# Tanh-capped attention and a gated MLP on one core: a new hand-written order of issue

## The chip, the cores and the metric

The kernel runs on one core of a Trainium2 chip. The metric is device time in microseconds, the median of several runs: 720.66 us for the kernel before (three runs, 720.16 to 720.66). Everything is float32; the products of the MLP use float32 split into two halves.

## What is computed

Attention over 8 batches, 12 heads, 448 positions and 64 columns per head, with scores capped by a tanh, and then an MLP whose gate mixes the positions:

```python
scores = cap * np.tanh(scale * np.matmul(q, k.transpose(0, 1, 3, 2)) / cap)
attn = np.exp(scores - np.max(scores, axis=-1, keepdims=True))
attn = attn / (np.sum(attn, axis=-1, keepdims=True) + 1e-09)
x = heads side by side of np.matmul(attn, v)        # 448 x 768 per batch
h = np.maximum(x @ w_in, 0.0); u, v = h[..., :512], h[..., 512:]
v_n = (v - mean(v)) / np.sqrt(var(v) + 1e-06)
v_s = np.einsum('ts,bsd->btd', w_spatial, v_n) + b_spatial[None, :, None]
out = (u * v_s) @ w_out
```

## The kernel before

The work is cut into 24 "quads" of four heads (three per batch) and 8 MLP batches. A function builds a list of 2823 steps (`plan.tasks`), each with an engine (T is TensorE, A ScalarE, V VectorE, P GpSimd, S the load queue on SyncE), the steps it depends on and the buffers it takes. Then a tuple, `ORDER`, lists the numbers of the steps in the order in which they are issued:

```python
    order = [plan.tasks[i] for i in ORDER] if bounded else plan.order()
    with tc.manual_schedule():
        for t in order:
            for u in t.allocs:
                make(u)
            t.fn()
```

Each engine works through its own steps strictly in that order; a step that waits (for another step's result, or for a buffer that is still in use) holds everything behind it on its engine. This holds for loads too: all of them are issued from SyncE, and a load whose buffer is not free holds the loads behind it.

What a quad does, by the names in the code (function `quad_bnd`): two raw loads (q and k of two head pairs, `raw`, four buffers) and two v loads; seven score steps `sc` (T, line 737, into one of two PSUM score banks `ps_s`); a `tanh` for each (A, line 741), which frees the bank; four exponentials `exp` (A, line 748); four `pv` steps (T, line 758, into the one `ps_x` bank), freed by a copy `xev` (A, line 764). VectorE folds the exponentials to a maximum (`red1`, `red2`, line 776; transpose 784; reduce `red3`, line 786). ScalarE shifts the result between partitions (`shift`, line 792), and small steps and loads over DRAM bring the reciprocals back. For the first four quads TensorE also sums the exponentials (`ones`, line 804). VectorE scales and splits the result into `xg` tiles (lines 839 and 489).

An MLP batch has 88 TensorE steps: u (lines 895 to 897), v (917 to 922), gate (986 to 991), output (1011 to 1013), with their copies and splits on ScalarE and VectorE. The output of the chip is stored by SyncE.

Weights come as int64 words and are converted on VectorE and ScalarE (`split_f64`, lines 555 to 569 and 489, 493): six steps behind each load. Blocks of w_in use one of three `w` buffers, and the first four of the six steps hold it; blocks of w_out use an `xg` buffer; rows of w_spatial come into one of three `wy` buffers (`split_f32`, load at line 514, cast at line 520). Before the list begins, the program has issued quad 0's raw loads and the first w_in block (lines 1043 to 1050), so steps 183, 184 and 0 issue nothing.

The numbers in `ORDER` that are spoken of later:

| number | step | engine |
|---|---|---|
| 7, 14, 21, 35 | loads of w_in blocks; 8 to 13, 15 to 20, 22 to 27 and 36 to 41 are the conversions | S; V, A |
| 18 | fourth conversion step of block 14 | V |
| 162, 169, 176 | loads of w_out blocks; 163 is the first conversion step of the first | S; V |
| 84, 85 | first load of w_spatial, its cast | S, V |
| 185, 186; 244 | v loads of quad 0; first v load of quad 1 | S |
| 242, 243; 301, 302 | raw loads of quad 1; of quad 2 | S |
| 246; 205 | first score step of quad 1; last one of quad 0 | T |
| 215, 216 | reduce of quad 0's maximum, its shift | V, A |
| 261, 265 | tanh 5 and 6 of quad 1 | A |
| 476, 480 | low half of batch 0's last gated tile; the output step that uses it | V, T |

Of the kernel before, what the change touches and what calls it, by code (L numbers as in the profile page):

```python
# [215 lines left out]
def gpc(n):  # L216
# [54 lines left out]
ORDER = (183, 184, 14, 0, 185, 187, 7, 186, 189, 188, 35, 243, 1, 242, 190, 2, 3, 191, 193, 195, 4, 15, 16, 17, 18, 84, 5, 194, 6,  # L271
# [137 lines left out]
def attn_moe(ctx, tc, bounded, shared, qk, v, qk2, v2, cap, w_in, w_sp, w_out, out):  # L409
# [613 lines left out]

    order = [plan.tasks[i] for i in ORDER] if bounded else plan.order()
    with tc.manual_schedule():
# [76 lines left out]
```

## Time and profile before

| | before |
|---|---|
| median of 3 runs | 720.66 us |
| profiled execution: its time, its span | 719.57 us, 717.3 us |
| TensorE busy | 706.5 us (98%) |
| VectorE busy | 594.6 us (83%) |
| ScalarE busy | 476.6 us (66%) |
| GpSimd busy | 25.8 us (4%) |
| granted TensorE clock | 1.00 |
| moved by DMA | 66.57 MB |

The span runs from the first to the last instruction of the profiled execution; a little lies around it. A busy time counts an engine's own instructions, waits left out. Matmuls overlap, so TensorE's steps are read by when they start. Starts in the views below are in microseconds from the start of the span.

### The profile page before, as it was taken

How to read it: one execution, taken by the hardware profiler on the slowest of the kernel's cores; microseconds unless marked ns; L12 is line 12 of the kernel's file. 1: busy time of each engine (PE TensorE's matmuls, PEld its weight loads, DVE VectorE, ACT ScalarE, POOL GpSimd, SP SyncE). 2: the span in 40 equal slices, each digit the busy share in tenths (PEclk: the TensorE clock that was granted, in tenths of full speed). 3: DMA queues.
4: the chain of work that ended last, by engine and by line, in shares of the span. 5: the costliest groups of instructions: out<-in, count | busy, mean ns of one | idle time of the engine just before them, and what ended most of it. 6: DMA issues, size and time to landing. Idle time of an engine off the chain costs nothing.

```text
span 717.3 us, 12273 instructions
## 1 busy us (share of the span) xinstructions
PE 706.5 (98%) x4954; PEld 483.0 (67%) x4954; DVE 594.6 (83%) x868; ACT 476.6 (66%) x646; POOL 25.8 (4%) x45
## 2 busy tenths in 40 slices
PE   8999999999999999999999999999999999999997
PEld 2334658665765958658676956667859666689896
DVE  6999999999999788999767499999768898793430
ACT  6999956787676576884475768687375874733321
POOL 0000010000200000000100010100000000000100
PEclk9999999999999999999999999999999999999999
DMA  8745415433031303323113411414104321202002
GB/s 288 245 135 175 164 42 161 126 104 119 12 104 52 130 9 122 93 76 118 51 42 89 155 37 57 141 52 128 66 27 116 103 71 48 65 1 79 27 1 82
DMA packets 34511, 66.57 MB, mean 93 GB/s; under 512 B 5995, under 2 KB 22156, under 8 KB 34444
## 3 DMA queue, kind: packets, MB, share of 16 engines
q1 hardware_dynamic: 34444, 65.68, 28.8%
q8 instruction: 41, 0.67, 0.4%
q14 instruction: 26, 0.21, 0.1%
HBM read 54.45 MB, written 11.18 MB: 92 GB/s over the span
## 4 chain that ended last, share of the span: by engine, by line
PE 79%; DVE 12%; ACT 7%; issue 1%; DMA 1%; ACTq 0%; DVEq 0%
PE ps_x L758 13%; PE ps_s L737 13%; PE ps_acc L895 4%; PE ps_acc L897 4%; PE ps_acc L896 4%; PE ps_acc L1011 4%; DVE red L776 4%; PE ps_acc L1012 4%; PE ps_acc L1013 4%; ACT tp L741 3%; PE ps_acc L920 3%; PE ps_acc L921 3%; PE ps_acc L922 3%; PE ps_acc L989 2%; ACT tp L748 2%; PE ps_acc L991 2%
## 5 line engine op out<-in xcount | busy, mean ns | idle before, releaser
L741 ACT ACTIVATE tp<-ps_s,capt 128x896 f32<-128x896 f32 x168 | 164.8, 1007 | 40.0 <-PE ps_s L737 36.1
L748 ACT ACTIVATE tp<-tp,capt 128x1792 f32<-128x1792 f32 x96 | 153.3, 1607 | 0.8
L737 PE MATMUL ps_s<-raw 64*64 64x448 f32 x1344 | 149.0, 545 | 3.0 <-ACT tp L741 2.9
L758 PE MATMUL ps_x<-tp,v 64*64 64x448 f32 x1344 | 141.2, 537 | 0.3 <-ACT xf L764 0.3
L776 DVE TENSOR_TENSOR red<-red,tp 128x1792 f32<-128x1792 f32 x88 | 136.3, 1549 | 5.5 <-ACT tp L748 3.7
L758 PEld LDWEIGHTS ps_x<-tp,v 64*64 64x64 f32 x1344 | 50.6, 133 | 76.0 <-issue 70.7
L737 PEld LDWEIGHTS ps_s<-raw 64*64 64x64 f32 x1344 | 46.7, 133 | 78.0 <-issue 41.9
L776 DVE TENSOR_TENSOR red<-tp 128x1792 f32<-128x1792 f32 x44 | 88.7, 2016 | 7.9 <-ACT tp L748 7.3
L895 PE MATMUL ps_acc<-xg,wi_h 128*128 128x448 f32 x180 | 66.2, 368 | 0.0
L897 PE MATMUL ps_acc<-xg,wi_l 128*128 128x448 f32 x180 | 65.2, 362 | 0.0
L896 PE MATMUL ps_acc<-xg,wi_h 128*128 128x448 f32 x180 | 65.0, 361 | 0.0
L1011 PE MATMUL ps_acc<-xg,wo_h 128*128 128x448 f32 x176 | 64.7, 368 | 0.0
L1012 PE MATMUL ps_acc<-xg,wo_h 128*128 128x448 f32 x176 | 63.8, 362 | 0.0
L1013 PE MATMUL ps_acc<-xg,wo_l 128*128 128x448 f32 x176 | 63.5, 361 | 0.0
L920 PE MATMUL ps_acc<-wi_h,xg 128*128 128x512 f32 x126 | 49.8, 395 | 0.1
L784 DVE STREAM_TRANSPOSE red<-red 128x896 f32<-128x896 f32 x44 | 48.6, 1104 | 0.9
L922 PE MATMUL ps_acc<-wi_h,xg 128*128 128x512 f32 x126 | 49.1, 390 | 0.0
L921 PE MATMUL ps_acc<-wi_l,xg 128*128 128x512 f32 x126 | 49.1, 390 | 0.0
L776 DVE TENSOR_TENSOR red<-red 128x896 f32<-128x896 f32 x44 | 47.8, 1087 | 0.5
L944 POOL TENSOR_TENSOR lst<-lst,capt 128x1 f32<-128x1 f32 x32 | 24.8, 782 | 650.5 <-DVE lst L942 570.1
L786 DVE TENSOR_REDUCE st<-red 128x28 f32<-128x896 f32 x44 | 47.5, 1079 | 0.6
L493 ACT COPY o<-ps_acc 128x448 f32<-128x448 f32 x44 | 23.2, 533 | 36.6 <-PE ps_acc L1013 34.0
(150 smaller groups left out, 1060.0 us busy)
## 6 DMA issues: line engine op xcount, KB each, us to landing
raw<-in_qk SPq DMA_DIRECT2D x46, 448.0 KB
rr<-rd SPq DMA_DIRECT2D x48, 224.0 KB
out<-o SPq DMA_DIRECT2D x48, 224.0 KB
v<-in_v SPq DMA_DIRECT2D x24, 256.0 KB
w<-in_w_in SPq DMA_DIRECT2D x11, 512.0 KB
v<-in_v SPq DMA_DIRECT2D x24, 192.0 KB
xg<-in_w_out SPq DMA_DIRECT2D x12, 256.0 KB
rd<-dt SPq DMA_DIRECT2D x48, 3.5 KB
```

What stands on the lines that cost most here:

```text
L737: nc.tensor.matmul(ps.t[c * D:(c + 1) * D, e, :S], lhsT=f(raw[c].t)[r, k:k + D], rhs=f(raw[c].t)[r, :S], start=True, stop=True)
L741: th = add("A", act(PW, 1), kk("th", i), lambda ps=ps, tp=tp, o=o: nc.scalar.activation(out=tp.t[:, o:o + PW].rearrange("p (e q) -> p e q" ...
L748: ex = add("A", act_s(w, 1), kk("ex", i), lambda tp=tp, w=w: nc.scalar.activation(out=tp.t[:, :w], in_=tp.t[:, :w], func=AF.Exp, scale=ca) ...
L758: nc.tensor.matmul(x.t[e * D:(e + 1) * D, c, :S], lhsT=vts[g // 2].t[c * D:(c + 1) * D, (4 * (g % 2) + 2 * j + e) * D:(4 * (g % 2) + 2 * j ...
L776: nc.vector.tensor_tensor(o_(), i0(), i1(), op=op)
L895: nc.tensor.matmul(ps, lhsT=wi1_h[:, c, fs], rhs=x[:, XH:], start=(c == 0), stop=False)
L896: nc.tensor.matmul(ps, lhsT=wi1_h[:, c, fs], rhs=x[:, :S], start=False, stop=False)
L897: nc.tensor.matmul(ps, lhsT=wi1_l[:, c, fs], rhs=x[:, XH:], start=False, stop=(c == NP - 1))
L920: nc.tensor.matmul(ps, lhsT=x[:, XH:][:, ts], rhs=wi2_h[:, c], start=(c == 0), stop=False)
L1011: nc.tensor.matmul(ps, lhsT=wo_h[:, c, ns], rhs=g[:, XH:], start=(c == 0), stop=False)
L1012: nc.tensor.matmul(ps, lhsT=wo_h[:, c, ns], rhs=g[:, :S], start=False, stop=False)
L1013: nc.tensor.matmul(ps, lhsT=wo_l[:, c, ns], rhs=g[:, XH:], start=False, stop=(c == 3))
```

## The change

One tuple is replaced. No step is added, removed or altered, no buffer and no load; all 2823 numbers stand in the new tuple once, in another order. All five engines are affected: 850 of TensorE's 984 places hold another step, 783 of VectorE's 861, 559 of ScalarE's 644, 263 of the load queue's 302, 24 of GpSimd's 32. The head of the diff, with the steps of the table above:

```diff
-ORDER = (183, 184, 14, 0, 185, 187, 7, 186, 189, 188, 35, 243, 1, 242, 190, 2, 3, 191, 193, 195, 4, 15, 16, 17, 18, 84, 5, 194, 6,
-    8, 196, 19, 197, 220, 192, 201, 199, 9, 10, 20, 11, 200, 202, 12, 221, 246, 205, 198, 36, 210, 37, 85, 38, 13, 39, 86, 203,
-    247, 206, 40, 248, 222, 252, 207, 249, 253, 21, 90, 244, 87, 28, 204, 258, 208, 254, 211, 41, 212, 91, 22, 92, 213, 23, 214,
-    24, 29, 215, 30, 88, 25, 31, 89, 250, 259, 255, 260, 223, 264, 279, 256, 224, 261, 26, 209, 262, 265, 216, 169, 301, 302, 49,
...
+ORDER = (162, 176, 169, 163, 183, 184, 187, 189, 188, 190, 191, 195, 193, 14, 0, 1, 164, 2, 165, 177, 3, 15, 166, 16, 4, 194, 196,
+    5, 17, 170, 18, 19, 185, 201, 192, 21, 199, 220, 197, 200, 202, 7, 186, 35, 178, 8, 6, 20, 9, 36, 10, 37, 11, 179, 203, 221,
+    243, 242, 246, 247, 205, 198, 206, 12, 252, 248, 204, 222, 302, 301, 244, 84, 38, 210, 85, 211, 86, 207, 249, 253, 254, 208,
+    258, 223, 250, 255, 209, 259, 256, 251, 264, 260, 279, 257, 39, 22, 212, 23, 213, 24, 13, 214, 25, 40, 215, 216, 26, 224, 261,
+    265, 245, 97, 28, 49, 218, 42, 307, 305, 262, 306, 217, 266, 98, 269, 171, 27, 41, 280, 281, 311, 90, 225, 282, 263, 87, 226,
...
```

## Rows read from the trace of the kernel before

**Rows 1.** Busy time by stretch: each engine's us (instructions), TensorE's granted clock, DMA share, GB/s.

```profile
7.20:40.00 32.80, 28.95 (x327) 10.03 (x322) 32.47 (x51) 32.47 (x35) 0.00 (x0) 1.00 0.71 248
35.00:40.00 5.00, 3.82 (x44) 1.31 (x40) 5.00 (x10) 4.90 (x8) 0.00 (x0) 1.00 0.16 55
40.00:138.47 98.47, 98.46 (x830) 56.96 (x823) 96.23 (x188) 81.81 (x115) 2.50 (x4) 1.00 0.45 141
138.47:250.00 111.53, 111.03 (x763) 76.85 (x762) 105.79 (x130) 77.91 (x107) 4.65 (x4) 1.00 0.28 88
250.00:600.00 350.00, 349.93 (x2449) 240.21 (x2448) 297.44 (x389) 240.46 (x317) 13.03 (x16) 1.00 0.26 81
600.00:712.00 112.00, 112.00 (x583) 96.71 (x581) 61.88 (x107) 41.94 (x72) 4.59 (x8) 1.00 0.12 40
```

**Rows 2.** Timeline of TensorE: start, us, line, operation; in brackets idle time before it.

```profile
28.69 0.98 PE L737 MATMUL ps_s<-raw 64*64 64x448 f32 x8
...
37.66 0.98 PE L737 MATMUL ps_s<-raw 64*64 64x448 f32 x8 [1.18 <-ACT tp L741]
```

**Rows 3.** Timeline of the load queue on SyncE: when loads are issued.

```profile
7.43 0.80 SPq L719 DMA_DIRECT2D raw<-in_qk  x2
8.34 0.37 SPq L514 DMA_DIRECT2D wy<-in_w_sp  x1
11.83 0.33 SPq L555 DMA_DIRECT2D w<-in_w_in  x1
19.53 0.33 SPq L514 DMA_DIRECT2D wy<-in_w_sp  x1
...
29.70 0.33 SPq L719 DMA_DIRECT2D raw<-in_qk  x1
```

**Rows 4.** GB/s moved in each microsecond from 0 to 40.

```profile
GB/s 0 0 75 141 369 415 377 430 377 344 379 346 283 390 394 413 392 37 0 0 108 310 309 281 145 264 378 415 417 395 233 309 136 134 321 242 19 0 0 16
```

**Rows 5.** Timeline of VectorE in the first 30 us.

```profile
7.20 0.43 DVE L562 TENSOR_SCALAR red<-red 128x512 f32<-128x512 f32 x1 [2.85 <-DMA red<-in_w_in]
7.66 0.43 DVE L566 TENSOR_SCALAR red<-red 128x512 uint32<-128x512 uint32 x1
...
11.11 0.69 DVE L569 SCALAR_TENSOR_TENSOR wy<-w,wy 128x512 uint32<-128x512 uint32 x1
11.72 0.68 DVE L489 TENSOR_TENSOR wi_l<-red,wi_h 128x512 fp32r<-128x512 f32 x1
...
17.91 0.39 DVE L520 CAST ws_h<-wy 128x448 fp32r<-128x448 f32 x1
...
20.56 2.02 DVE L776 TENSOR_TENSOR red<-red,tp 128x1792 f32<-128x1792 f32 x1
...
24.40 0.43 DVE L562 TENSOR_SCALAR wy<-w 128x512 f32<-128x512 f32 x1
24.73 0.62 DVE L489 TENSOR_TENSOR ws_l<-wy,ws_h 128x448 fp32r<-128x448 f32 x1
...
28.54 1.08 DVE L786 TENSOR_REDUCE st<-red 128x28 f32<-128x896 f32 x1
```

**Rows 6.** Timelines of VectorE and TensorE at the end of batch 0.

```profile
137.86 0.61 DVE L489 TENSOR_TENSOR xg<-o,xg 128x448 fp32r<-128x448 f32 x1
...
139.11 0.36 PE L1011 MATMUL ps_acc<-xg,wo_h 128*128 128x448 f32 x1
139.32 0.36 PE L1012 MATMUL ps_acc<-xg,wo_h 128*128 128x448 f32 x1
```

**Rows 7.** Timeline of TensorE at two changes of kind of work.

```profile
48.02 1.68 PE L737 MATMUL ps_s<-raw 64*64 64x448 f32 x16
49.53 1.68 PE L758 MATMUL ps_x<-tp,v 64*64 64x448 f32 x16
...
58.28 1.73 PE L737 MATMUL ps_s<-raw 64*64 64x448 f32 x16
59.94 0.47 PE L895 MATMUL ps_acc<-xg,wi_h 128*128 128x448 f32 x1
```

243 rows, old and new, of the table ORDER are left out of this document.

## The prediction

> **What bounds the kernel now.** I read the busy time by stretch first [rows 1]. From 40 us to the last matmul TensorE is busy in 98.46 of 98.47, 111.03 of 111.53, 349.93 of 350.00 and 112.00 of 112.00 us, at a granted clock of 1.00 throughout. No new order can make that part shorter by more than these few tenths. The only stretch with room is the start: 28.95 of 32.80 us between 7.20 and 40, so 3.85 us in all, the longest hole being the 1.18 us ahead of 37.66, where TensorE waits for the tanh that frees a score bank [rows 2]. The same table shows who sets the pace there: ScalarE and VectorE are each busy 32.47 of 32.80 us. VectorE stays the fullest engine behind TensorE up to 138.47 (96.23 of 98.47 us) [rows 1]. So VectorE is idle for 0.33 + 2.24 = 2.57 us between 7.20 and 138.47. The reader is to see two things: hardly anything can be gained after 40 us, and a hole torn into VectorE's work before 138 us can hardly be filled again.
>
> Whether such a hole costs time depends on how late VectorE delivers. At the end of batch 0 it writes the low half of the last gated tile (step 476) from 137.86 for 0.61 us, so until 138.47. TensorE enters the step that uses it (480) at 139.11 and reads the low half with its second matmul at 139.32 [rows 6]. The slack is 0.85 us. I compared the two tables at this place: exactly the same 235 VectorE steps stand ahead of 476, and exactly the same 158 TensorE steps ahead of 480. Whatever idle time VectorE gains up to there reaches TensorE less 0.85 us, and behind it TensorE has nothing to win it back from.
>
> **The change, part by part.** *Middle and end.* The same steps in other runs. Changes of TensorE between attention and MLP go from 47 to 49, one pair more. Two score steps took 1.51 us between attention steps (48.02 to 49.53) and 1.66 us ahead of an MLP run (58.28 to 59.94) [rows 7]; the pair costs twice 0.15 at most, and I take 0.2 us. Up to 250 us VectorE has 5.74 us idle behind 138.47, and 52.56 us between 250 and 600 [rows 1], which covers what is swapped there. The last steps are again an output projection, its copy and its store. I count nothing else here; a new wait of a microsecond is possible and lies in the range.
>
> *The head of the load queue.* Two lines of the trace show how this queue acts. The fourth load of a w_in block (a transfer into `w`) was issued at 11.83, just when VectorE's fourth operation on an earlier block ended (11.11 + 0.69 = 11.80): there are three such buffers, and SyncE stands until one is free. The load of quad 3's q and k at 29.70 came just when quad 1's last scores ended (28.69 + 0.98 = 29.67): there are four raw buffers [rows 2, 3, 5]. In the table of before, quad 1's raw loads (243, 242) and the first w_spatial load (84) stand ahead of that fourth w_in load; they went out at 7.43 and 8.34 [rows 3]. In the new table three w_out blocks (162, 176, 169) come first, then w_in blocks 14, 21, 7, and the fourth w_in load (35) ahead of quad 1's raws. Quad 2's raws (302, 301) come next, and the w_spatial load 84 only behind them and quad 1's first v.
>
> *What VectorE meets.* I follow its new queue with the start-to-start times of the rows: 0.33 us for a 512-column operation between unrelated ones (24.40 to 24.73), 0.61 for the two-input one (11.11 to 11.72), for the 256-column ones somewhat over half of that (0.2 and 0.33, estimates), 2.02 for a first fold. Sizes are the code's: a w_out block 262 KB, a w_in block 524, raw 459, w_spatial 229, v 262 or 197. Bytes come from the rate row: with the queue full it sums to 1377 KB by 7 us, 1807 by 8, 2528 by 10, 2907 by 11 and 4320 by 15 us. The start loads are 1442 KB, and their first 1180 KB (reached at 6.5) let VectorE start at 7.20, 0.7 later [rows 4, 5].
> 1. VectorE's first step is now 163, on a w_out block: 1442 + 262 = 1704 KB, reached at 7.8, so a start at 8.4 instead of 7.20. Hole 1.2.
> 2. Step 15 needs block 14, now behind 786 KB of w_out: 2752 KB, 10.6 + 0.7 = 11.3; VectorE is there at 10.65. Hole 0.6.
> 3. Step 18, which frees the buffer for load 35, ends at 14.4 (11.80 before). Step 8 waits for block 7 (4062 KB, 15.0): hole 0.5. Load 35 goes out at 14.4; after an issue at 19.53 on an idle queue bytes flowed from about 20.7 [rows 3, 4], so its 524 KB flow from 15.6 to 17.0 at 380 KB/us, and step 36 starts at 17.7: hole 0.8.
> 4. Quad 1's raws (918 KB) follow until 19.4, so the first score step of quad 1 (246) starts at 20.0. Quad 0's last scores (205) stand behind it on TensorE: 20.75 to 21.75. Only then do quad 2's raws get their buffers; they go out at 21.8, flow from 23.0, and with v and load 84 (1409 KB) end at 26.7. Step 85, the cast of that w_spatial block, starts at 27.4. It stands in VectorE's queue directly behind quad 0's first fold, which ends at 22.4. Hole 5.0. In before, 85 ran at 17.91 with no wait [rows 5].
>
> The holes sum to 1.2 + 0.6 + 0.5 + 0.8 + 5.0 = 8.1 us. Against that, the new queue mixes two chains, so that a step seldom follows its own predecessor: 0.46 us start to start in a chain (7.20 to 7.66) against 0.33, and eight such neighbours before step 36 go away: 8 x 0.13 = 1.0. VectorE is later by 7.1 us.
>
> *Who waits for that.* Behind 85 stand the rest of quad 0's maximum, whose end (step 215, at 29.62 in before, 9.06 us after 20.56 [rows 5]) moves to about 37. ScalarE has the shift of that result (216) in front of quad 1's tanh 5 and 6 now, behind them before; so quad 1's last tanhs and the score bank that quad 2's first scores need come about 38 to 40 us. TensorE stands some 4 us there. That is the same delay seen from another engine, not added.
>
> The sum: 7.1 - 0.85 + 0.2 = about 6.4 us. The profiled execution took 719.57 us with a span of 717.3; it becomes 726.0 with a span of 723.7. The median of the runs shown is 1.09 us above the profiled execution, and I forecast on it: 720.66 + 6.4 = 727.0. Low end of this case: all 2.57 us of VectorE's old idle time fill up, 3.8 us, 724.5. High end: quad 2's transfers flow at the 281 KB/us of the slice at 23 us [rows 4] rather than 380, 5.0 instead of 3.7 us, 728.3.
>
> **The clock.** Before, the granted clock is 1.00 in the stretch from 35 to 40 too, where TensorE was busy 3.82 of 5.00 us [rows 1]; a hole as long as the new one stands in no row. [...]
>
> **The rivals.** *Faster.* If loads and holes were as before, the new order would lead ScalarE past one w_in cast less, and the tanhs ahead of some exponentials, before quad 2's scores: banks come free earlier, and of TensorE's 3.85 us of holes about half could go, 2 us: 718.7. It decides when step 84 lands before VectorE is at 85, that is by 22.4. Against it: two buffer waits in a row, both seen in the trace. *No change.* The same delay exists, but VectorE has made it up before 138: 720.7. It needs the hole at 85 to be under about 2 us, so a landing near 24; the rate row leaves no room for 1.4 MB between 21.8 and 24. [...]
>
> **How the numbers follow.** Forecast 0.73 (724.5 to 728.3), slower still 0.12, no change 0.08, faster 0.07. Two executions of this kernel can be told apart from about 0.2%, 1.4 us. So faster 0.07, same 0.08, slower 0.85. The range 723.0 to 731.0 takes in the forecast's bounds and the slower rival, and leaves out the other two.
>
> **What the new profile would show.** VectorE's first operation near 8.4 on `xg`; the fourth `w` load issued near 14.4; quad 2's raws near 21.8; VectorE idle some 5 us at the line of the cast of `wy` (520), ended by a DMA; ScalarE idle some 4 us at line 792, and TensorE idle as long before 40 us. From 45 us on TensorE is full again, step 476 ends near 145, and the rest is only shifted. Wrong would be: step 85 without a wait (then the queue doesn't hold loads as I read it); or that wait with the end of 476 near 139 (then VectorE had cover that I don't see); or a full start and a new hole after 140.

## The result and the profile after

The changed kernel takes 729.91 us, median of five runs (728.54 to 731.85), against 720.66 (720.16 to 720.90, five runs): a ratio of 1.0132, 95% interval 1.0118 to 1.0145. That is 9.25 us slower; the forecast was 6.4 us (727.0), with a range of 723 to 731. The forecast's own case was bounded by 724.5 and 728.3; 729.91 lies above it, in the part of the range that was drawn for the rival "slower still". The profiled execution took 731.43 us with a span of 729.5, against 719.57 and 717.3. It is the second slowest of the five, so the views below show a loss of 11.86 us where the medians differ by 9.25.

The busy time by stretch, in the columns of [rows 1]:

```profile
7.20:40.00 32.80, 24.85 (x262) 8.76 (x256) 20.18 (x37) 23.58 (x23) 0.00 (x0) 0.90 0.52 179
40.00:150.00 110.00, 105.92 (x884) 59.04 (x881) 107.33 (x200) 90.39 (x126) 2.39 (x4) 0.97 0.47 147
150.00:250.00 100.00, 99.92 (x709) 66.76 (x708) 96.00 (x122) 71.13 (x92) 3.08 (x4) 1.00 0.28 89
250.00:600.00 350.00, 349.87 (x2394) 245.60 (x2396) 298.78 (x388) 237.72 (x319) 9.44 (x16) 1.00 0.27 81
600.00:712.00 112.00, 112.00 (x637) 90.70 (x630) 74.45 (x119) 48.30 (x81) 4.40 (x8) 1.00 0.13 40
```

From 150 us on TensorE is as full as before. The first stretch has changed: VectorE worked 32.47 us in it and now 20.18, ScalarE 32.47 and now 23.58, TensorE 28.95 and now 24.85.

VectorE's own timeline shows where it stood (the number in brackets is the idle time ahead of the operation, and what ended it; most operations without a wait are left out):

```profile
8.53 0.29 DVE L562 TENSOR_SCALAR xg<-xg 128x256 f32<-128x256 f32 x1 [4.21 <-DMA xg<-in_w_out]
...
11.72 0.43 DVE L562 TENSOR_SCALAR wy<-w 128x512 f32<-128x512 f32 x1 [0.88 <-DMA w<-in_w_in]
...
16.00 0.43 DVE L562 TENSOR_SCALAR wy<-w 128x512 f32<-128x512 f32 x1 [0.97 <-DMA w<-in_w_in]
...
20.15 0.43 DVE L562 TENSOR_SCALAR wy<-w 128x512 f32<-128x512 f32 x1 [2.18 <-DMA w<-in_w_in]
...
22.96 2.02 DVE L776 TENSOR_TENSOR red<-tp 128x1792 f32<-128x1792 f32 x1
32.24 0.39 DVE L520 CAST ws_h<-wy 128x448 fp32r<-128x448 f32 x1 [7.25 <-DMA wy<-in_w_sp]
...
41.10 1.12 DVE L786 TENSOR_REDUCE st<-red 128x28 f32<-128x896 f32 x1
```

Every one of the waits shown ends with a transfer; of the operations in [rows 5] only the first, at 7.20, has a wait ahead of it, the cast of line 520 at 17.91 none. Besides the start (8.53 for 7.20) the holes are 0.88, 0.97, 2.18 and 7.25 us. The load queue, in the columns of [rows 3], and the GB/s of each microsecond from 0 to 40, as in [rows 4]:

```profile
14.85 0.33 SPq L555 DMA_DIRECT2D w<-in_w_in  x1
15.27 11.48 SPq L719 DMA_DIRECT2D raw<-in_qk  x4
27.66 0.33 SPq L726 DMA_DIRECT2D v<-in_v  x1
28.08 0.38 SPq L514 DMA_DIRECT2D wy<-in_w_sp  x1
```

```profile
GB/s 0 0 72 156 375 417 369 414 350 365 346 334 297 383 331 91 239 319 288 304 212 54 4 0 0 0 32 240 391 366 302 79 0 16 178 18 0 0 0 0
```

Load 35 goes out at 14.85, quad 1's raws right behind it, quad 2's raws not before some 26 (the group of four issues stretches from 15.27 to 26.75), and the w_spatial load 84 at 28.08. Between 22 and 26 us next to nothing is moved: the transfers are not slow there, the queue stands.

TensorE and ScalarE at the same place, and the granted clock around it:

```profile
22.67 3.27 PE L737 MATMUL ps_s<-raw 64*64 64x448 f32 x16 [4.48 <-DMA raw<-in_qk]
25.68 1.92 PE L758 MATMUL ps_x<-tp,v 64*64 64x448 f32 x16
...
44.32 3.26 PE L737 MATMUL ps_s<-raw 64*64 64x448 f32 x16 [4.01 <-ACT tp L741]
```

```profile
42.25 0.22 ACT L792 COPY sh<-st 32x32 f32<-32x32 f32 x1 [4.69 <-DVE st L786]
```

```profile
18.00:26.00 8.00, 3.52 (x24) 1.45 (x24) 4.84 (x7) 3.75 (x4) 0.00 (x0) 0.58 0.31 108
26.00:40.00 14.00, 13.91 (x160) 5.03 (x152) 7.76 (x11) 10.83 (x11) 0.00 (x0) 1.00 0.36 116
40.00:50.00 10.00, 5.99 (x48) 2.13 (x48) 9.74 (x12) 6.84 (x10) 0.00 (x0) 0.66 0.77 245
```

TensorE has two holes of over 4 us, and over the two score steps behind each the granted clock is 0.50 (from 22.67 to 25.68 and from 44.32 to 47.51; the means of 18 to 26 and of 40 to 50 us are 0.58 and 0.66): two score steps take 3.01 us from start to start (22.67 to 25.68), where two took 1.51 in [rows 7]. The end of batch 0, and TensorE's busy time on the way there:

```profile
150.04 0.64 DVE L489 TENSOR_TENSOR xg<-o,xg 128x448 fp32r<-128x448 f32 x1
```

```profile
151.00 0.36 PE L1011 MATMUL ps_acc<-xg,wo_h 128*128 128x448 f32 x1
151.20 0.36 PE L1012 MATMUL ps_acc<-xg,wo_h 128*128 128x448 f32 x1
```

```profile
72.00:150.00 78.00, 78.00 (x588) 49.39 (x585) 77.39 (x154) 62.51 (x91) 2.39 (x4) 1.00 0.44 136
```

Against [rows 6] step 476 ends 12.21 us later (150.68 for 138.47) and TensorE reads it 11.88 later (151.20 for 139.32). At the end the span is 12.2 us longer. From 72 us TensorE is busy without a hole, so it was as late at 72 us already: the whole loss is made in the head.

### The profile page after: what moved, and what is told of

It is laid out like the page before. It is cut to its first block, busy times and chain, and to the rows that moved or that the text cites. A ratio compares the mean times of both kernels' runs of the same rounds, so it can differ in the third digit from the quotient of the medians.

```text
span 729.5 us, 12311 instructions
## 1 busy us (share of the span) xinstructions
PE 710.5 (97%) x4954; PEld 484.1 (66%) x4954; DVE 597.5 (82%) x868; ACT 476.1 (65%) x646; POOL 20.3 (3%) x45
## 4 chain that ended last, share of the span: by engine, by line
PE 84%; DVE 8%; ACT 3%; DMA 2%; issue 1%; SPq 0%; ACTq 0%; DVEq 0%
PE ps_s L737 15%; PE ps_x L758 15%; PE ps_acc L895 5%; PE ps_acc L897 5%; PE ps_acc L896 5%; PE ps_acc L1011 4%; PE ps_acc L1012 4%; PE ps_acc L1013 4%; DVE red L776 4%; PE ps_acc L920 3%; PE ps_acc L921 3%; PE ps_acc L922 3%; PE ps_acc L989 3%; PE ps_acc L991 2%; PE ps_acc L990 2%; PE ps_acc L917 1%
## 5 line engine op out<-in xcount | busy, mean ns | idle before, releaser
L737 PE MATMUL ps_s<-raw 64*64 64x448 f32 x1344 | 150.0, 552 | 10.8 <-ACT tp L741 6.2
L748 ACT ACTIVATE tp<-tp,capt 128x1792 f32<-128x1792 f32 (+1 forms) x96 | 153.0, 1607 | 0.8
L493 ACT CAST xg<-xf 128x448 fp32r<-128x448 f32 (+1 forms) x96 | 35.3, 408 | 22.6 <-DVE xf L839 15.8
```

The source lines that it names most:

```text
L737: nc.tensor.matmul(ps.t[c * D:(c + 1) * D, e, :S], lhsT=f(raw[c].t)[r, k:k + D], rhs=f(raw[c].t)[r, :S], start=True, stop=True)
L748: ex = add("A", act_s(w, 1), kk("ex", i), lambda tp=tp, w=w: nc.scalar.activation(out=tp.t[:, :w], in_=tp.t[:, :w], func=AF.Exp, scale=ca) ...
```

## The experiments

The theory (A) is that of the forecast: VectorE's holes behind held loads in the head make the loss. The rivals are that the rest of the new table makes it, tried first, and that TensorE's and ScalarE's own holes and the clock make it; each text on record says which of them it calls B. All ratios are to the kernel before, run beside each kernel on the same chip; the chips differ from run to run (the kernel before took 720.66 to 721.65 us on them), so kernels are compared by their ratios. In the short diffs of loads, numbers stand in the order in which SyncE issues them.

**Which part of the table.** Up to the end of batch 0's gate both tables issue the same 638 steps (159 of TensorE, 236 of VectorE, 148 of ScalarE, 91 loads, 4 of GpSimd). So the head can be taken from one and the rest from the other.

```diff
-ORDER = (new head, new rest)
+ORDER = (these 638 in the old order, new rest)   # old_head_new_rest
+ORDER = (these 638 in the new order, old rest)   # new_head_old_rest
```

> Every engine runs the order of before up to the end of batch 0's gate (236 VectorE steps, 159 TensorE, 148 ScalarE, 91 loads) and the new order from there. Theory A (the whole loss is made in the first 55 us, by the load queue): 720.7 within 1.5 us, TensorE full from 40 us on as in before. Theory B (part of the loss comes from the new runs in the middle): above 723, with new holes of TensorE behind 140 us.

> The other half: the new order up to the end of batch 0's gate, the old order from there. Theory A: as slow as the changed kernel, 729 to 732, with the same 7 us wait of VectorE for a wy load near 25 to 32 us. Theory B: clearly under 728.

Measured: the old head with the new rest 719.73 us, 0.9976 (0.9964 to 0.9988); the new head with the old rest 730.51 us, 1.0129 (1.0092 to 1.0166). Both fall where theory A put them: the head alone makes the loss; the rest costs nothing that can be told. VectorE's busy time from 7.2 to 60 us, old head first (columns as in [rows 1]):

```profile
7.20:60.00 52.80, 48.39 (x555) 17.57 (x553) 50.83 (x81) 52.01 (x59) 0.00 (x0) 1.00 0.66 221
```

```profile
7.20:60.00 52.80, 41.88 (x426) 14.39 (x424) 39.64 (x66) 40.71 (x43) 0.00 (x0) 0.90 0.57 184
```

**One load at a time.** Both kernels are the changed one with loads moved ahead of load 35.

```diff
-35, 243, 242, 302, 301, 244, 84
+84, 35, 243, 242, 302, 301, 244   # load84_first
+243, 242, 35, 302, 301, 244, 84   # raws_first
```

> The new order with one load moved: the first w_spatial load (84) goes out ahead of the fourth w_in load (35); nothing else changes. If the wait of step 85 for that load is the main term (7.25 of about 12 us), VectorE has no wait at line 520, ScalarE's 4.7 us wait at line 792 and TensorE's 4.0 us hole near 40 us go away: about 724 to 725. If the late raw loads of quad 1 (TensorE's 4.5 us hole at 18 us) are the main term and 85 only follows them, the time stays above 727.

> The new order with quad 1's two raw loads (243, 242) moved ahead of load 35; load 84 stays behind quad 2's raws. Quad 1's first scores should start near 16.5 instead of 22.7, with no hole of 4.5 us and no half clock there; quad 2's raws go out near 18 instead of 26, so load 84 lands some 6 to 7 us earlier too and the wait at line 520 shrinks to under 1.5 us. Theory A, with the raws as the root: 721 to 723. If 85's wait for 84 is a cause of its own that stays: about 725.

Measured: 724.94 us, 1.0043 (1.0025 to 1.0060), and 725.51 us, 1.0052 (1.0035 to 1.0070). Each move takes away 60 to 70% of the loss. With 84 first the time is in the range given for it; VectorE casts 84 without a wait, ScalarE's wait at line 792 and TensorE's hole near 40 us are gone, and TensorE's hole ahead of quad 1 stays. With the raws first, that hole shrinks to 0.56 us, and waits behind 84 stay, shorter. There the 721 to 723 of theory A fell and the other case, "about 725", came: quad 1's scores started at 19.17 for the 16.5 expected, quad 2's raws went out at 20.93 for 18, and the wait at line 520 is 1.99 us for under 1.5. VectorE and TensorE with 84 first:

```profile
25.28 0.38 DVE L520 CAST ws_h<-wy 128x448 fp32r<-128x448 f32 x1
```

```profile
22.70 3.27 PE L737 MATMUL ps_s<-raw 64*64 64x448 f32 x16 [4.34 <-DMA raw<-in_qk]
```

VectorE, ScalarE and TensorE with the raws first:

```profile
27.12 0.40 DVE L520 CAST ws_h<-wy 128x448 fp32r<-128x448 f32 x1 [1.99 <-DMA wy<-in_w_sp]
```

```profile
37.09 0.22 ACT L792 COPY sh<-st 32x32 f32<-32x32 f32 x1 [4.38 <-DVE st L786]
```

```profile
19.17 1.73 PE L737 MATMUL ps_s<-raw 64*64 64x448 f32 x16 [0.56 <-DMA raw<-in_qk]
...
39.16 3.27 PE L737 MATMUL ps_s<-raw 64*64 64x448 f32 x16 [3.70 <-ACT tp L741]
```

**Both moves.**

```diff
-35, 243, 242, 302, 301, 244, 84
+243, 242, 84, 35, 302, 301, 244
```

> The new table with both moves of the two earlier runs: q1's raw loads 243 and 242 and then the w_spatial load 84 go out ahead of load 35; nothing else differs. Theory A (VectorE's holes behind held loads make the loss): the 7.25 us before the cast at L520 and the 2.2 us before load 35's cast go or shrink below 1, what stays is the 1.33 + 0.88 us behind the first w_in and w_out blocks and about 1 us: 3.2 less the slack of 0.85 over the 719.7 of the old head with the new rest, so about 722 (720.5 to 723). Theory B (TensorE's and ScalarE's own holes and the clock make it): no wait at L792, no hole at 40 us and no half clock are left, so 719.5 to 720.5. If something else in the new head costs (a third cause), it stays at 724 to 725.5, where each move alone left it.

Measured: 722.96 us, 1.0032 (1.0017 to 1.0046), just within the range of theory A (720.5 to 723) and outside that of B. This doesn't refute B, though: its range supposed that no hole is left near 40 us, and ScalarE still waits 2.55 us at line 792 and TensorE 1.86 us behind it. Another point missed: the hole at load 35 did not shrink, it is 2.61 us, behind the 1.1 MB that now stand ahead of that load. VectorE and TensorE:

```profile
20.57 0.43 DVE L562 TENSOR_SCALAR wy<-w 128x512 f32<-128x512 f32 x1 [2.61 <-DMA w<-in_w_in]
```

```profile
37.35 2.11 PE L737 MATMUL ps_s<-raw 64*64 64x448 f32 x16 [1.86 <-ACT tp L741]
```

**ScalarE's order alone.** The shift 216, which waits for VectorE, goes behind tanh 5 and 6 again, first in the changed kernel, then in the one with the raws first.

```diff
-216, 26, 224, 261, 265, 245
+26, 224, 261, 265, 216, 245
```

> The new table with one step moved: ScalarE's copy 216 (L792), which waits for VectorE's step 215, goes behind the tanh steps 261 and 265 again; all loads stay as the change has them. Under both theories ScalarE's 4.7 us wait ahead of tanh 5, TensorE's 4.0 us hole at 40 us and the half clock behind it go. Theory A: VectorE's holes (1.33, 0.88, 0.97, 2.18, 7.25) stay, its step ahead of the gate ends as late as before, and the time stays at 728 to 730.5. Theory B: 4.0 us of hole and 1.6 us of scores at half clock come off, 723.5 to 725.

> The run with q1's raws first (725.5), and copy 216 behind the tanh steps 261 and 265 as well. There VectorE's wait at L520 had shrunk to 1.99 us, but ScalarE still waited 4.38 us at L792 and TensorE 3.70 us behind it, at half clock for 3.41 us after. Theory A: VectorE's waits (1.3, 0.9, 1.9, 2.0, together 6.1 less 0.85 of slack over 719.7) are the loss that is left: 724.5 to 726. Theory B: 3.7 + 1.6 come off: 720 to 721.5.

Measured: 727.80 us, 1.0112 (1.0089 to 1.0136) against 1.0132 (1.0118 to 1.0145) without the move, and 723.88 us, 1.0053 (1.0037 to 1.0068) against 1.0052. The first is within theory A (728 to 730.5) but for 0.2 us, and 2.8 above what B gave at most; whether some 1 to 2 us are gained can't be told, as the intervals overlap. The second shows no gain by its ratio; its 723.88 us lie in neither range, 0.6 below that of A. The two runs don't decide between the theories, because the holes that both expected to go did not: TensorE still waits 2.62 us in the first kernel and 2.11 in the second. Taking the copy out of the way only moves ScalarE's wait to the next step that needs VectorE (TensorE in the first kernel, ScalarE in the second):

```profile
40.07 2.73 PE L737 MATMUL ps_s<-raw 64*64 64x448 f32 x16 [2.62 <-ACT tp L741]
```

```profile
35.58 0.62 ACT L493 CAST wi_h<-wy 128x512 fp32r<-128x512 f32 x1 [3.04 <-DVE wy L569]
```

**The clock alone.** In the kernel with load 84 first, 16 matmuls are added ahead of quad 1's first scores.

```diff
             def scores(i=i, ps=ps):
+                for _ in range(16 if turn == 1 and i == 0 else 0):
+                    nc.tensor.matmul(ps.t[:, 0, :D + 80], lhsT=busy[:, 16:], rhs=busy, start=True, stop=True)
                 for c in range(2):
```

> Prices the granted clock by itself: the run with load 84 first (724.9, where the only hole of TensorE left is the 4.34 us ahead of q1's first scores, with the clock at half behind it) and 16 matmuls of 128x128 on 144 columns of ones, added ahead of that score step, into the bank that the scores then overwrite. They should fill some 4 of the 4.34 us. If an idle TensorE is what lowers the clock, the granted clock stays at 1.0 from 18 to 26 us and the two score steps take 1.6 us each where they took 3.27 and 3: q1's work is 1.5 to 3 us earlier. Is that price on the path, 721.9 to 723.5; is VectorE ahead of it all the while (theory A), the clock stays up and the time stays at 724 to 725.5. If the clock falls all the same, idleness isn't what lowers it.

Measured: 723.89 us, 1.0043 (1.0029 to 1.0058), the very ratio without them; in microseconds it falls between the two ranges. They did what they were for (the 16 matmuls stand as 32 records in the trace, and the added lines of code make line 737 of before 741, and 758 762). TensorE and the clock:

```profile
18.06 4.19 PE L737 MATMUL ps_s<-one 128*128 128x144 f32 x32
22.18 1.73 PE L741 MATMUL ps_s<-raw 64*64 64x448 f32 x16
23.74 1.68 PE L762 MATMUL ps_x<-tp,v 64*64 64x448 f32 x16
```

```profile
18.00:26.00 8.00, 8.00 (x78) 5.56 (x78) 6.52 (x9) 5.47 (x7) 0.00 (x0) 1.00 0.48 154
```

The clock stays at 1.00 where it was 0.57, the score steps take 1.56 us where they took 3.01, and the time doesn't change beyond its interval. So an idle TensorE is what lowers the clock here. What that costs the kernel isn't settled: by the two intervals a gain of some 1.6 us could hide, as much as the scores gained. The profiled execution is 1.80 us faster than that of load84_first, but there VectorE also waited 1.25 us less for load 35 (1.49 for 2.74), at 19.5 us and so ahead of quad 1's scores.

**The third edit of the head.** In the kernel with both moves, the three w_out loads and ten of their conversions (163 to 166, 170, 171, 177 to 180) go behind quad 1's loads and VectorE's step 271.

```diff
-162, 176, 169, 183, 184, 14, 0, 185, 21, 7, 186, 243, 242, 84, 35, 302, 301, 244, 245, 97
+183, 184, 14, 0, 185, 21, 7, 186, 243, 242, 84, 35, 302, 301, 244, 245, 162, 169, 176, 97
```

> The run with both moves (q1's raws and load 84 ahead of load 35; ratio 1.0032), and the head's third edit taken back: the three w_out loads 162, 169 and 176 go out behind q1's values instead of first of all, and ten of their conversion steps, 163 to 180, follow step 271 on VectorE instead of standing between the first w_in steps. Theory A, with time going by VectorE's holes less a slack of 0.85: its first step starts at 7.2 us and not at 8.5, the hole behind the first w_in block goes, 1.9 to 2.7 us in all, and load 35, which waits for step 18, comes earlier too: ratio 0.998 to 1.0005, as with the old head. Theory B (holes of the other engines, or the order of TensorE's steps in the new head by itself): the time stays where it was, 1.002 to 1.004.

Measured: 722.37 us, 1.0018 (1.0007 to 1.0029). It missed theory A's numbers; its interval reaches into B's range (1.002 to 1.004), and against the 1.0032 (1.0017 to 1.0046) of both moves no gain can be told. VectorE starts at 7.56, but comes to the next transfers the earlier, and waits there:

```profile
14.04 0.45 DVE L562 TENSOR_SCALAR wy<-w 128x512 f32<-128x512 f32 x1 [1.78 <-DMA w<-in_w_in]
...
19.76 0.43 DVE L562 TENSOR_SCALAR wy<-w 128x512 f32<-128x512 f32 x1 [3.73 <-DMA w<-in_w_in]
```

**Load 35 ahead again.** From the last kernel, 35 goes back ahead of quad 1's raws.

```diff
-243, 242, 84, 35
+35, 243, 242, 84
```

> The kernel of wout_late (1.0018) with load 35 back ahead of q1's raws 243 and 242 and of 84, so that the load queue has the order of the kernel before (35, 243, 242, 84, then q2's raws), while TensorE, VectorE and ScalarE keep the new head's order apart from the ten w_out steps. In wout_late the new wait of 3.73 us was for load 35, which went out at 12.29 behind 1.1 MB of other transfers and was used at 19.76. Theory A: ahead of them it lands by 16, that hole shrinks to below 1 us, the 1.78 us behind the first w_in block stays, the cast of 84 stands later than its landing: VectorE misses some 3 us less the slack of 0.85, ratio 0.9995 to 1.002. Theory B (the other engines' order in the new head costs by itself): 1.0018 or above, though the loads have their old order.

The text on record is wrong in one point: this is not the old queue. There the fourth w_in load, the one that waits for a buffer, is 21 and stands behind the raws and 84; here it is 35, ahead of them, as in the change. So the edit puts the hold back, and the number, though B's words ("1.0018 or above") cover it, doesn't decide for B. Measured: 724.96 us, 1.0056 (1.0042 to 1.0069) against 1.0018 (1.0007 to 1.0029): the hold costs again, 0.38% or some 2.7 us. Load queue, TensorE and VectorE:

```profile
13.60 0.33 SPq L555 DMA_DIRECT2D w<-in_w_in  x1
14.10 1.81 SPq L719 DMA_DIRECT2D raw<-in_qk  x2
```

```profile
20.68 2.41 PE L737 MATMUL ps_s<-raw 64*64 64x448 f32 x16 [3.75 <-DMA raw<-in_qk]
```

```profile
38.13 0.39 DVE L531 CAST ws_l<-wy 33x448 fp32r<-33x448 f32 x1 [5.28 <-DMA wy<-in_w_sp]
```

The raws went out at 7.92 in wout_late and at 14.10 here. A second loss came with it, the last line's 5.28 us ahead of the cast of load 97, a late part of w_spatial.

**That last hole.** Load 97 stood behind the three w_out loads that I had moved, so these now go behind it.

```diff
-244, 245, 162, 169, 176, 97, 28, 49
+244, 97, 245, 28, 162, 169, 176, 49
```

> The kernel of old_load_order (profiled 726.77, its longest hole the 5.28 us at L531, the cast of load 97, a part of w_spatial of 58 KB that went out at 34.27 behind the three moved w_out loads) with these three behind 97 and 28, and 97 ahead of q1's second values, 245; nothing else. It is a forecast by the rule that the ten profiled executions so far fit: time = 719.33 (the old head with the new rest) + what VectorE works less than its 50.83 us from 7.2 to 60 us - 0.85 of slack. 97 waits for step 13 (about 29 us) and lands some 3 us later, so the 5.28 us shrink to 0.5 to 1.5 and VectorE's missing work from 8.38 to 3.9 to 4.6 us: profiled 722.4 to 723.1, ratio 1.0015 to 1.0035. Theory B (what the other engines' order costs by itself): no change, 724 to 727.

Measured: 724.39 us, 1.0044 (1.0028 to 1.0059); against 1.0056 no difference can be told, and against the 1.0018 of wout_late the hold still costs some 0.26%. The hole at line 531 is gone, and VectorE waits for ScalarE's exponentials instead:

```profile
35.71 2.03 DVE L776 TENSOR_TENSOR red<-tp 128x1792 f32<-128x1792 f32 x1 [3.29 <-ACT tp L748]
```

These come late, since quad 1 started at 20.11, behind a hole of 3.67 us for its held raws, with the granted clock at 0.57 from 18 to 26 us. So here VectorE's wait goes back to TensorE's late scores. My forecast of its time (722.4 to 723.1) fell, and the time is where B put it (724 to 727). The rule below holds for it too, as the next table shows: VectorE misses 6.78 us of work, not the 3.9 to 4.6 that I took.

**What all of them have in common.** In every profiled execution I set what VectorE works less than 50.83 us (the old head with the new rest) between 7.2 and 60 us beside the time above that kernel's profiled 719.33. The names: shift_late and raws_shift_late are the two kernels of "ScalarE's order alone", both_loads_first that of "Both moves", load84_busy that of "The clock alone"; wout_late, old_load_order and old_loads_97 are the last three, in their order.

| kernel | VectorE busy 7.2 to 60, us | work missing, us | profiled time, us | above 719.33, us |
|---|---|---|---|---|
| the change | 38.60 | 12.23 | 731.43 | 12.10 |
| new head, old rest | 39.64 | 11.19 | 731.22 | 11.89 |
| old_load_order | 42.45 | 8.38 | 726.77 | 7.44 |
| shift_late | 43.05 | 7.78 | 726.40 | 7.07 |
| old_loads_97 | 44.05 | 6.78 | 724.86 | 5.53 |
| raws_first | 44.33 | 6.50 | 725.24 | 5.91 |
| load84_first | 44.58 | 6.25 | 724.39 | 5.06 |
| raws_shift_late | 45.73 | 5.10 | 723.00 | 3.67 |
| both_loads_first | 45.85 | 4.98 | 722.96 | 3.63 |
| wout_late | 46.12 | 4.71 | 722.68 | 3.35 |
| load84_busy | 46.66 | 4.17 | 722.59 | 3.26 |

The time follows the missing work, less 0.1 to 1.4 us (in one case 0.7 more than it); the slack of step 476 in the forecast was 0.85. Whatever starved VectorE in these kernels (a held load, transfers that share the rate, late exponentials), about as much time was lost. The table can't say that VectorE is the engine that carries the loss. ScalarE's missing work in the same stretch, against the 52.01 us of the old head, follows the time about as closely: 12.39 us in the change, 6.12 with 84 first, 5.02 with both loads first, 3.88 in load84_busy. The one run that changes TensorE's work alone, load84_busy, is too small a step to decide it, so which of the three engines carries the loss stays open. What the moved loads show is that the order of the load queue makes most of the loss: 1.0132 goes to 1.0032 by moving three loads and nothing else. The 0.5% between that and the old head is not taken apart.

**The best of them once more.**

> The kernel of old_head_new_rest a second time, on another chip and in more executions, since its gain was near the limit of what can be told: ratio 0.9964 to 0.9988 to before if the new order behind the head is worth the 0.24% it showed; 0.9985 to 1.0005 if that gain was in the executions of before on that one chip.

Measured: 719.85 us (719.14 to 720.55, twelve runs), 0.9986 (0.9975 to 0.9997), after 0.9976. It ran on the same chip as the first time, not on another one as the text says, and 0.9986 lies in both ranges; so whether the gain holds on other chips isn't shown. On this one the old head with the new rest beats the kernel before by 0.1 to 0.25%. No view of the profile shows where: the spans of its two profiled executions are 717.1 and 717.5 us, that of before 717.3. The executions of before reach from 719.18 to 722.97 there; why the new rest keeps them closer together stays open.

## Why the prediction was right, and where a size was off

- *TensorE is full behind 40 us, and what is lost ahead of 138 is not made up.* Right, but for the hole of 4.01 us that ends at 44.32: the lag of 12 us is there by 72 us and stays, and with the head put back the time is back.
- *Where the lost time reaches TensorE: the step that failed.* The prediction has VectorE's delay reach TensorE at the end of batch 0, through step 476, less a slack of 0.85. In the profile that wait does not occur: step 476 ends at 150.68, TensorE reads the tile at 151.20, and from 72 to 150 us it is busy 78.00 of 78.00 us. TensorE was late already, through its own holes of 4.48 and 4.01 us in the head and the slow steps behind them. Over the whole span it is idle 8.2 us more than before (729.5 - 710.5 = 19.0, for 717.3 - 706.5 = 10.8) and busy 4.0 us more with the same steps. The hole at 40 us, which the prediction saw as the same delay from another engine and did not add, is itself 4.01 of the 12.2 us. Both holes go back to the held loads, as VectorE's do; so a sum along VectorE could come near the loss although the delay doesn't reach TensorE where the prediction has it, and in that the number is luck. The slack of 0.85 took no part here (the lag is 12.21 us at VectorE's step and 11.88 at TensorE's, with no wait between them).
- *Middle and end, +0.2 us.* Of the wrong sign, and small: with the old head the new rest gains some 1 to 1.7 us; with the new head (1.0132 for 1.0129) no gain can be told. Nothing in the rows of before let me see it.
- *The head of the queue.* Right as a mechanism: VectorE's first operation on `xg` at 8.53 (forecast 8.4), load 35 at 14.85 (14.4), a wait at the cast on line 520 ended by a DMA, ScalarE's wait at line 792 of 4.69 us (about 4), TensorE's of 4.01 us (some 4). The runs with one load moved, and the one that put the hold back, show that the held loads make most of the loss.
- *Hole 3, load 35: the first term that was mis-sized.* Forecast 0.5 + 0.8, measured 0.97 + 2.18. I let its 524 KB flow alone from 15.6 to 17.0. The rate row moves 1241 KB from 15 to 20 us, when its block is first used at 20.15; load 35 and the 918 KB of raws issued from 15.27 are 1442 KB. So the bytes of transfers issued within a microsecond seem to have come together and not one after the other; that is read from the sums and wasn't tried by itself. The rate was lower too: 239 to 319 KB in each microsecond from 16 to 20, where I took the 380 of a full queue.
- *Hole 4, load 84: the second.* Forecast 5.0, measured 7.25, at 32.24 for 27.4. Quad 1's scores started at 22.67 for 20.0 (their raws shared that slower rate with load 35), and these and quad 0's last ones took 3.01 us for some 1.5, at a granted clock of 0.50, so quad 2's raws followed some 4 us late. VectorE's first fold ended 2.6 us later than forecast (24.98 for 22.4), which leaves 2.25 us more of a hole.
- *The clock.* The rival "slower still" had 0.12, and the range was drawn beyond 728.3 for it. No run shows how many microseconds it was worth: in the rows of before the granted clock is 1.00 in every stretch, so that size was an estimate of mine alone. What the runs showed in its place: over the two score steps behind the hole of 4.48 us the granted clock is 0.50 (0.58 from 18 to 26), and they took 3.01 us, against 1.51 in [rows 7], and 1.56 with the hole filled and the clock at 1.00. So the clock did fall, behind both holes and together with the forecast's mechanism, and the measured 729.91 is nearer to the range's upper end of 731.0 than to the forecast's 727.0. That the measured time lies within 723.0 to 731.0 is owed to this rival; two of the five executions (731.43, 731.85) lie above it. With the first hole filled no gain was measured, but one as large as this price could hide in the intervals.
- *The sum.* 1.33 + 0.88 + 0.97 + 2.18 + 7.25 = 12.6 us of holes for 8.1. The discount of 1.0 for mixed chains can't be seen beside them (12.23 of work missing). With 12.6 in place of 8.1 and the other terms as they were, the prediction's own sum (12.6 - 1.0 - 0.85 + 0.2) would give some 11 us; the profiled execution lost 11.86, and step 476 ended at 150.68 for "near 145".
- *No change* and *faster* fell with the first point: the cast of 84 waited 7.25 us, and a landing by 24 us was never in reach.

## What to carry to other kernels

Where the engine behind the bound one is as full as its neighbour (here 32.47 of 32.80 us at the start), a new order of issue is judged first by the load queue: for each load in it, which buffer does it wait for, and who behind it is needed sooner? A load that waits for a buffer holds all loads behind it: putting load 35 back ahead of quad 1's raws cost 0.38%. Whether the w_out blocks at the very front cost time could not be told here (1.0032 with them in front, 1.0018 without, with overlapping intervals). When a new order is judged, take head and rest apart: here the rest was a small gain on the one chip, and the head cost several times as much.

## What the runs showed of the hardware that I had not expected

The granted clock falls behind shorter holes than the two of over 4 us, but not behind each. With both loads moved, a hole of 1.86 us ahead of 37.35 is followed by a clock of 0.50; with the w_out loads late, a hole of 1.88 us ahead of 36.20 is followed by 1.00. The first kernel's stretch, then the second's:

```profile
40.00:42.00 2.00, 2.00 (x25) 0.98 (x20) 2.00 (x3) 1.95 (x4) 0.00 (x0) 0.50 0.72 163
```

```profile
38.00:42.00 4.00, 3.68 (x60) 1.48 (x60) 3.68 (x5) 3.95 (x6) 0.00 (x0) 1.00 0.74 210
```

In the first the slow steps were the sums at line 804 (39.40 to 42.45 for 32 matmuls; with the w_out loads late the same 32 took from 38.02 to 39.68), while the clock from 37 to 39 us, where the scores right behind the hole ran, had a mean of 0.97. So the fall came a few steps behind its hole. What tells the two apart is open.
